# A fused attention and MLP-mixer kernel on one core: six reloaded weight slots, 56 score blocks, small passes on GpSimd, and a first chunk in half-chunks

## The chip, the core and the metric

The kernel runs on one core of a Trainium2 chip. The core has five engines, each with its own queue: TensorE (PE; its weight loads are listed apart as PEld), VectorE (DVE), ScalarE (ACT), GpSimd (POOL) and SyncE (SP, which here only issues DMAs). PE writes to eight PSUM banks of 128x512 float32 each; the other engines read these and work in SBUF. The metric is the device time of one execution in microseconds, the median of several.

## What is computed

One input x (2048 tokens of 512 features, bfloat16) goes through an attention block (a) and an MLP-mixer block (b); a sigmoid gate per token mixes the two.

```python
def reference(A_x, A_wqkv, A_wo, B_x, B_w1, B_w2, B_w3, B_w4, gate_w):
    ...
        scores = jnp.einsum("bhqd,bhkd->bhqk", q, k) * (Dh ** -0.5)
        p = _softmax(scores, axis=-1)
        o = jnp.einsum("bhqk,bhkd->bhqd", p, v)
        return (lambda x, *d: x.transpose(*d))(o, 0, 2, 1, 3).reshape(B, S, D) @ wo
    ...
        h = _gelu(_layernorm(x, axis=-1) @ w1)
        ...
        hs = jnp.concatenate([g0, g1, g2, g3], axis=-1) @ w2
        x1 = x + hs
        h2 = _gelu(_layernorm(x1, axis=-1) @ w3) @ w4
        return x1 + h2
    ...
    g = _sigmoid((x * gate_w).sum(-1, keepdims=True))
    a = _A_ref(x, A_wqkv, A_wo)
    b = _B_ref(x, B_w1, B_w2, B_w3, B_w4)
    return g * a + (1 - g) * b
```

There are 32 heads of 16 features. g0 to g3 are the four quarters of h, shifted by 1, -1, 2 and -2 tokens. w3 is 512x1792, w4 is 1792x512.

## The kernel before, in words

The 2048 query tokens are four chunks of 512. A round is one chunk, one group G of eight heads and one parity p: four heads at a time, one on each strip of 32 rows of PE. A round has 64 score blocks: 16 key tiles of 128 tokens for each of four heads, each block 128 keys by 512 queries, made by one matmul (L1482) with kT as its weights and q as the moving side. q is kept twice, with the odd heads zeroed (scaled by mE) and with the even heads zeroed (scaled by mO), since two heads share a strip. There are 32 rounds, 2048 blocks in all.

Each block must become exp(score). There are two ways. On ACT (`issue_act`, L1565) an exponential reads two or three PSUM banks at once and writes bfloat16 to `prob`, a pool of 40 slots of 128x512 (L1577). On DVE (`issue_dve`, L1589) the block is scaled and rounded to an integer whose bits are a rough exponential (L1609); three copies of it with a constant added to the bits (the shift passes) follow, on DVE (L1652) or GpSimd (L1654), and four PV matmuls, with V or with V scaled, add up to a better one. So a block costs PE one PV matmul (L1707) if it went to ACT and four if it went to DVE.

The projections and the MLP are cut into matmuls on four strips of 32 columns (L1112, from `gen`) and are fed between the score blocks. The results are copied out of PSUM by DVE (`evac`). Layernorm is bn_stats on DVE (L1284), a power on GpSimd, a normalising pass xn on DVE (L1304), a write to DRAM (L1308) and transposing DMAs back (L1314). GELU runs on ACT in three places (L1324): once over the whole of hT, and twice over hB and hT for a pair of chunks; each needs a table load there and one back.

The order of all this is worked out in the kernel while it is built. `Sim` holds a model of the engines and hands out work by priorities, buffers and planned positions, all counted in score blocks (`at`, the P_ constants, and STEPS, a table of parameters that can change every 8 blocks). What comes out is a fixed program for each engine; on the chip, the engines wait for one another by semaphores only, and each keeps its order. Buffers come from pools: `w` has nine slots of 128x4x512 for transposed x, the k and v weights, w1, w2, w3 (four slots), w4 (four slots) and the last outputs `ybuf`; wo has a tile of its own. `port=True` marks work that the planner keeps from overlapping between DVE and GpSimd; GpSimd then also waits for the last such DVE instruction.

The steps that the change touches: the loads of x and of the weights (`start`, `wload`, `load_xT`), the first chunk's transposes, q and k (`x_transposes`, `k_first`, `q_proj`), the q copies in `q_proj` (L1210), xn in `normalise`, the gate scaling of x_sb in `mlp2_up` (L1366), w3 and w4 in `mlp2_up` and `mlp2_down`, and the tail behind the last PV matmul (L2052 to L2103).

## Time and profile before

| | us |
|---|---|
| median of 3 runs (lowest, highest) | 735.15 (734.89, 735.43) |
| the profiled execution | 735.27 |
| its span in the profile | 733.3 |
| DMA: HBM read, written | 17.40 MB, 6.81 MB |
| granted TensorE clock | 0.999 |

In the groups of instructions a line gives the line of the code, the engine, the operation, what it writes and reads with shapes, the count, then the engine's busy time and the mean duration of one in ns, then the idle time of the engine just before them and what ended it. Neighbouring instructions of an engine overlap in the records, so busy time divided by the count is less than the mean duration. A line of the timeline gives start, duration, engine, line and the number of instructions merged into it. A line of the waits gives total time, number of waits and the longest. A line of the stretches gives for each engine the busy time and the number of instructions, then the granted clock, the DMA engines' share and GB/s.

### The profile page before, as it was taken

The numbers are of one execution on the slowest core, as the hardware profiler recorded it, in microseconds if no ns is written. First come the engines' busy times: TensorE is split into PE (matmuls) and PEld (weight loads), VectorE is DVE, ScalarE is ACT, GpSimd is POOL, SyncE is SP. The second block draws the span as 40 slices with busy tenths as digits, with TensorE's granted clock in tenths as the row PEclk, the third lists the DMA queues.
The fourth block names the chain that finished last, engine by engine and source line by source line (L and its number), as shares of the span: only waits on it lengthen the run. The fifth ranks groups of instructions, "written<-read, shape, count | busy, mean of one in ns | idle before, by whom it ended". The sixth has DMA issues, their size and how long they took to land.

```text
span 733.3 us, 23826 instructions
## 1 busy us (share of the span) xinstructions
PE 723.8 (99%) x9517; PEld 212.3 (29%) x9518; DVE 698.6 (95%) x1493; ACT 720.0 (98%) x751; POOL 452.7 (62%) x452
## 2 busy tenths in 40 slices
PE   9999999999999999999999999999999999999997
PEld 5434322222222222222322222222222232222222
DVE  6999999999999999999999999999999999999997
ACT  7999999999999999999999999999999999999995
POOL 3456685778867666658545555566576765575442
PEclk9999999999999999999999999999999999999999
DMA  8504223111212033024100100001100010000001
GB/s 189 162 19 77 80 66 71 28 45 57 72 49 53 21 96 69 21 81 96 32 25 10 46 28 21 27 23 43 27 20 18 7 32 24 28 26 19 14 22 41
DMA packets 67094, 34.60 MB, mean 47 GB/s; under 512 B 46748, under 2 KB 62380, under 8 KB 66984
## 3 DMA queue, kind: packets, MB, share of 16 engines
q1 hardware_dynamic: 66040, 32.56, 17.7%
q8 instruction: 74, 1.21, 0.7%
q10 hardware_dynamic: 944, 0.52, 0.2%
q14 instruction: 36, 0.29, 0.2%
HBM read 17.40 MB, written 6.81 MB: 33 GB/s over the span
## 4 chain that ended last, share of the span: by engine, by line
PE 64%; ACT 11%; DVE 4%; issue 2%; POOL 0%; ACTq 0%; DVEq 0%
PE banks L1707 24%; PE banks L1482 22%; PE banks L1112 17%; ACT prob L1577 6%; ACT hT L1324 2%; ACT hB L1324 2%; DVE prob L1609 1%; DVE prob L1652 1%; ACT L1324 1%; DVE x_sb L1357 0%; ACT L1326 0%; DVE st L1284 0%; DVE w L1415 0%; POOL prob L1654 0%; PE banks L2060 0%
## 5 line engine op out<-in xcount | busy, mean ns | idle before, releaser
L1577 ACT ACTIVATE prob<-banks 128x1024 bf16<-128x1024 f32 (+1 forms) x728 | 675.5, 1102 | 1.1 <-PE banks L1482 0.2
L1654 POOL TENSOR_SCALAR prob<-prob 128x1024 uint16<-128x1024 uint16 x390 | 400.3, 1045 | 233.4 <-DVE prob L1652 110.9
L1609 DVE TENSOR_SCALAR prob<-banks 128x512 uint16<-128x512 f32 x577 | 380.3, 684 | 17.4 <-PE banks L1482 12.9
L1707 PE MATMUL banks<-prob,V 128*17 128x512 bf16 (+1 forms) x3785 | 321.6, 381 | 0.2
L1482 PE MATMUL banks<-q,kT 32*128 32x512 bf16 x2048 | 280.1, 384 | 1.5 <-ACT prob L1577 0.7
L1652 DVE TENSOR_SCALAR prob<-prob 128x1024 uint16<-128x1024 uint16 x480 | 179.5, 422 | 2.0 <-PE banks L1707 0.6
L1482 PEld LDWEIGHTS <-kT 32*128 32x128 bf16 x2048 | 70.0, 90 | 295.3 <-ACT prob L1577 269.2
L1707 PEld LDWEIGHTS <-V 128*17 128x17 bf16 (+1 forms) x3785 | 71.8, 88 | 116.7 <-issue 94.9
L1112 PE MATMUL banks<-xnT,w 128*32 128x512 bf16 x1152 | 89.4, 383 | 0.0
L1112 PE MATMUL banks<-w,hT 128*32 128x512 bf16 x688 | 64.5, 384 | 0.0
L1746 POOL TENSOR_TENSOR oT<-accsb,bcs 128x512 bf16<-128x512 f32 x31 | 39.5, 1273 | 26.7 <-DVE prob L1652 21.5
L1112 PEld LDWEIGHTS <-w 128*32 128x32 bf16 x1936 | 41.0, 95 | 48.9 <-issue 27.0
L1112 PE MATMUL banks<-w,w 128*32 128x256 bf16 (+1 forms) x784 | 41.5, 308 | 0.4 <-DVE prob L1609 0.4
L1112 PE MATMUL banks<-w,hB 128*32 128x512 bf16 x448 | 36.0, 382 | 0.6 <-ACT hB L1324 0.6
L1123 PE MATMUL banks<-wo,oD 32*128 32x512 bf16 x64 | 24.6, 384 | 0.0
L1112 PEld LDWEIGHTS <-hT 128*32 128x32 bf16 x688 | 15.9, 95 | 20.5 <-issue 15.1
L1284 DVE BATCH_NORM_STATS2 st<-x_sb 128x6 f32<-128x512 bf16 x32 | 21.5, 678 | 0.0
L1728 DVE COPY accsb<-banks 128x512 f32<-128x512 f32 x31 | 21.1, 680 | 0.2 <-PE banks L1707 0.2
L1112 PE MATMUL banks<-wo,oD 128*32 128x512 bf16 x176 | 21.0, 384 | 0.0
L1112 PE MATMUL banks<-w,wq 128*32 128x512 bf16 x256 | 19.4, 382 | 1.0 <-DVE accsb L1728 1.0
L1378 DVE CAST hB<-banks 128x512 bf16<-128x512 f32 x28 | 19.0, 682 | 0.9 <-PE banks L1112 0.9
L1324 ACT ACTIVATE hT<-hT 128x7168 bf16<-128x7168 bf16 (+1 forms) x3 | 19.4, 6452 | 0.0
(94 smaller groups left out, 246.8 us busy)
## 6 DMA issues: line engine op xcount, KB each, us to landing
bcs<-rr SPq DMA_DIRECT2D x124, 64.0 KB
xn_dram<-xn SPq DMA_DIRECT2D x32, 128.0 KB
w<-in_B_w_dram SPq DMA_DIRECT2D x5, 512.0 KB
oD<-oT SPq DMA_DIRECT2D x124, 16.0 KB
w<-in_B_w_dram SPq DMA_DIRECT2D x4, 448.0 KB
out_dram<-ot SPq DMA_DIRECT2D x14, 128.0 KB
x_sb<-in_A_x_dram SPq DMA_DIRECT2D x3, 512.0 KB
w<-in_A_wqkv_dram SPq DMA_DIRECT2D x2, 256.0 KB
```

The costliest lines, as they stand in the source:

```text
L1112: units.append([Op("col", j, lambda j=j, lf=lf, rf=rf, n0=n0, n1=n1, st=st, sp=sp: nc.tensor.matmul(get()[32 * j:32 * j + 32, n0:n1], lhsT ...
L1123: o = Op("row", i, lambda: nc.tensor.matmul(get(), lhsT=lf(0, P)[rows], rhs=rf()[rows], start=False, stop=True, tile_position=(32 * i, 0), ...
L1284: a = dve(600, deps, lambda: nc.vector.bn_stats(out=sb.slot[:], in_=x_sb[:, t, :]), prio=6, at=at, acq=[sb])
L1324: g = nc.scalar.activation(out=ap, in_=ap, func=ACT.Gelu_apprx_tanh)
L1482: o = Op("row", i, lambda: nc.tensor.matmul(dst(), lhsT=kT[G][32 * i:32 * i + 32, kt * P:(kt + 1) * P], rhs=qbuf[G, c].slot[32 * i:32 * i ...
L1577: job = act(hold, ops, lambda: nc.scalar.activation(out=prob[:, pb.cut(), :].bitcast(BF16), in_=unit()[:, rb.cut(), :], func=ACT.Exp, scal ...
L1609: return nc.vector.tensor_scalar(out=prob[:, b0.cut() if w == 2 else b0.bufs[h0].slot, :], in0=unit()[:, rb.cut() if w == 2 else rb.bufs[0 ...
L1652: return nc.vector.tensor_scalar(out=cut(k), in0=cut(0), scalar1=float(SHIFT * k), scalar2=None, op0=ALU.add)
L1654: return nc.gpsimd.tensor_scalar(out=cut(k), in0=cut(0 if both else 2), scalar1=1.0, scalar2=float(SHIFT * (k if both else 1)), op0=ALU.mu ...
L1707: return nc.tensor.matmul(one(accs[r])[32 * i:32 * i + n, :], lhsT=lhs(n), rhs=rhs(), start=st and not edge, stop=True, tile_position=(0, ...
L1728: e = dve(PSUM_NS, round_ops[r], lambda: nc.vector.tensor_copy(out=ab.slot[:], in_=one(accs[r])), acq=[ab], prio=0, frees=[accs[r], Call(a ...
L1746: n = gp(1250, d3, lambda: nc.gpsimd.tensor_tensor(out=ob.slot[:], in0=ab.slot[:], in1=bb.slot[:], op=ALU.mult), acq=[ob], frees=[ab, bb], ...
```

## The change

1. `w` has six slots in place of nine, `prob` 56 in place of 40. wo moves into a `w` slot, loaded late; w2 is loaded late; w3 and w4 are loaded once for each pair of chunks and not once for all, so that they take turns in four slots; `ybuf` moves into an `xnT` slot.
2. The two q copies of each q projection (30), the xn passes (32) and the gate scalings of x_sb (14) move from DVE to GpSimd.
3. x's first chunk comes in four loads of one row tile each, two on SP and two on ACT, where there were two loads of two. A new function `first` does its transposes, copies, q and k in halves of 256 tokens by hand, with k and q on the whole array and not on four strips, after nine warm-up matmuls in place of eleven.
4. In the tail the matmuls on known data all stand behind the last PV matmul, the last four row tiles of the output leave from one `w` slot, the first two of them in one DMA.
5. Assumed latencies of DMAs and GELUs in the planner, planned positions and the table STEPS are others. In the program that comes out, ACT has 657 exponentials of two blocks and 48 of three (715 and 13 before), DVE 590 blocks (579), GpSimd 364 shift passes (390).

```diff
-    P_W1 = (143, 440)
+    P_W1 = (195, 445)
...
-    P_W3 = ((610, 710), (710, 840), (1200, 1390), (1400, 1570))
+    P_W3 = ((610, 710), (710, 840), (1245, 1400), (1410, 1570))
...
-    P_LD = (450, 888)
+    P_LD = ((450, 1190), (845, 1575))
...
-    NPROB, NTOK, NW = 40, 3, 9
+    NPROB, NTOK, NW = 56, 5, 6
...
-    xa, xb = (start(e, 3000.0, lambda q, a=a: q.dma_start(out=x_sb[:, a:a + 2, :], in_=x_src(0, a, a + 2)))
-              for e, a in (("SP", 0), ("ACT", 2)))
-    j_x0 = [xa, xb]
+    j_x0 = [start(("SP", "ACT")[a % 2], 3000.0, lambda q, a=a: q.dma_start(out=x_sb[:, a, :], in_=x_flat[a * P:(a + 1) * P, :]))
+            for a in range(4)]
...
-        dl_w[name] = dma(4000.0, [], fn, acq=[wslot(name, users)], prio=2)
+        dl_w[name] = dma(6300.0, [], fn, acq=[b], prio=2)
...
-    dl_w["o"] = dma(4000.0, [], lambda: nc.sync.dma_start(out=wo[:], in_=wrows(A_wo)), prio=2)
+    dl_w["2"].at = 330
+    wload("o", A_wo, 10 ** 6)
+    dl_w["o"].at = 855
...
-        for _ in range(11):
+        for _ in range(9):
...
+    def first(t):
...
+        def project(b, w, n0):
+            for k in range(KT):
+                guard(b, nc.tensor.matmul(one(b)[:, 0:256], lhsT=w[:, k, 0:P], rhs=W("x00")[:, k, n0:n0 + 256], start=k == 0,
+                                          stop=k == KT - 1, skip_group_check=True))
+
+        def mm():
+            parts = [(bt[0], 0, 0, 2), (bt[1], 0, 2, 4), (bt[2], 2, 0, 2), (bt[3], 2, 2, 3), (bt[4], 2, 3, 4)]
+            for i, (b, t0, k0, k1) in enumerate(parts):
+                for k in range(k0, k1):
+                    for u in range(2):
+                        guard(b, nc.tensor.transpose(
+                            out=one(b).bitcast(BF16)[:, (k - k0) * 256 + u * P:(k - k0) * 256 + (u + 1) * P],
+                            in_=x_sb[:, t0 + u, k * P:(k + 1) * P], identity=idb[:]))
+            for i, (b, t0, k0, k1) in enumerate(parts):
+                cp = nc.scalar.copy if i in (1, 3) else nc.vector.tensor_copy
+                sim.readers[b] = [cp(out=W("x00")[:, k0:k1, t0 * P:(t0 + 2) * P], in_=one(b).bitcast(BF16)[
+                    :, 0:(k1 - k0) * 256].rearrange("p (k c) -> p k c", c=256))]
+            project(bq[0], wq, 0)
+            nc.scalar.activation(out=qb.slot[:, 0, 0:256], in_=one(bq[0])[:, 0:256], func=ACT.Copy, scale=mE[:])
+            project(ba, W("k"), 0)
+            sim.readers[ba] = [nc.vector.tensor_copy(out=kT[0][:, 0:256], in_=one(ba)[:, 0:256])]
+            project(bq[1], wq, 256)
+            nc.vector.tensor_scalar(out=qb.slot[:, 0, 256:512], in0=one(bq[1])[:, 0:256], scalar1=mE[:], scalar2=None,
+                                    op0=ALU.mult)
+            project(bb, W("k"), 256)
...
-            j_q[G, c, p] = dve(262, [e, j_m3] + ([j_q[G, c, 0]] if p else []), lambda p=p, m=m: nc.vector.tensor_scalar(
-                out=qb.slot[:, p, :], in0=qf.slot[:], scalar1=m[:], scalar2=None, op0=ALU.mult), prio=0.3, port=True,
+            j_q[G, c, p] = gp(690, [e, j_m3] + ([j_q[G, c, 0]] if p else []), lambda p=p, m=m: nc.gpsimd.tensor_scalar(
+                out=qb.slot[:, p, :], in0=qf.slot[:], scalar1=m[:], scalar2=0.0, op0=ALU.mult, op1=ALU.add), prio=0.3,
                 acq=[] if p else [qb], frees=[qf])
...
-            g = dve(323, [m], lambda t=t, xb=xb: nc.vector.tensor_scalar(
+            g = gp(750, [m], lambda t=t, xb=xb: nc.gpsimd.tensor_scalar(
                 out=xb.slot[:], in0=x_sb[:, t, :], scalar1=rs[which][:, t:t + 1], scalar2=nm[which][:, t:t + 1],
...
-            jx1g[t] = dve(262, [last[t % 4], jgate], lambda t=t: nc.vector.tensor_scalar(
...
+            jx1g[t] = gp(700, [last[t % 4], jgate], lambda t=t: nc.gpsimd.tensor_scalar(
...
-    for i in range(KT):
-        wload(f"3{i}", B_w3[i * P:(i + 1) * P, :], NCH * FT)
...
+    for cs, at3, at4 in zip(PAIRS, *P_LD):
+        for i in range(KT):
+            wload(f"3{i}", B_w3[i * P:(i + 1) * P, :], 2 * FT)
+            dl_w[f"3{i}"].prio, dl_w[f"3{i}"].at = 6, at3 + 10 * i
+        for i in range(4):
+            wload(f"4{i}", B_w4[512 * i:min(F, 512 * (i + 1)), :], 8)
+            dl_w[f"4{i}"].prio, dl_w[f"4{i}"].at = 7, at4 + 10 * i
         mlp2(cs, s2, at_of, gate_job)
...
     for tt in (1, 3):
-        add_y(tt, tt not in early)
-    for tt in range(4):
-        if tt not in early:
-            known(tt, range(LG, 4), tt % 2 == 0)
+        into(tt, idf[:], y_of(tt), True)
+        known(tt, False)
+        known(tt - 1, True)
...
-        (nc.scalar if tt == 3 else nc.sync).dma_start(out=out_flat[t * P:(t + 1) * P, :], in_=o[:])
+        if tt == 1:
+            nc.sync.dma_start(out=out_flat[(t - 1) * P:(t + 1) * P, :].rearrange("(t p) d -> p t d", p=P), in_=both[:, 0:2, :])
+        elif tt > 1:
+            (nc.scalar if tt == 3 else nc.sync).dma_start(out=out_flat[t * P:(t + 1) * P, :], in_=o)
```

819 lines of the change are left out of this document (413 added, 406 removed).

## The prediction

> **What bounds the kernel now.** I read the busy times first. Four engines look full, so busy time alone decides nothing.
>
> ```profile
> PE 723.8 (99%) x9517; PEld 212.3 (29%) x9518; DVE 698.6 (95%) x1493; ACT 720.0 (98%) x751; POOL 452.7 (62%) x452
> ```
>
> Then the groups of instructions, for ScalarE (ACT). Its exponentials are one line of code in two widths, 1024 columns (two score blocks) and 1536 (three).
>
> ```profile
> L1577 ACT ACTIVATE prob<-banks 128x1024 bf16<-128x1024 f32 (+1 forms) x728 | 675.5, 1102 | 1.1 <-PE banks L1482 0.2
> L1577 ACT ACTIVATE prob<-banks 128x1024 bf16<-128x1024 f32 x715 | 659.7, 1095 | 0.8 <-PE banks L1482 0.2 <-DVE prob L1652 0.2 <-ACT prob L1577 0.2
> L1577 ACT ACTIVATE prob<-banks 128x1536 bf16<-128x1536 f32 x13 | 19.3, 1487 | 0.2
> L1324 ACT ACTIVATE hB<-hB 128x7168 bf16<-128x7168 bf16 x2 | 12.4, 6177 | 0.0
> L1324 ACT ACTIVATE hT<-hT 128x8192 bf16<-128x8192 bf16 x1 | 7.0, 7032 | 0.0
> ```
>
> Before 728 exponentials ACT is idle for 1.1 us in all. Busy can still hide waiting, so I checked the rate in stretches without a GELU, then who waits for whom, then the two ends.
>
> ```profile
> 200.00:300.00 100.00, 99.92 (x1291) 27.62 (x1287) 96.85 (x213) 99.84 (x109) 68.89 (x70) 1.00 0.23 56
> 400.00:500.00 100.00, 99.92 (x1266) 26.61 (x1263) 97.59 (x209) 99.84 (x109) 56.15 (x53) 1.00 0.11 30
> PEld L1482 <- ACT prob L1577: 269.2, 645, 0.8
> 8.54 8.28 ACT L1577 ACTIVATE prob<-banks 128x1536 bf16<-128x1536 f32 x7
> 715.83 8.82 ACT L1577 ACTIVATE prob<-banks 128x1024 bf16<-128x1024 f32 x9
> 728.71 0.69 ACT L2099 ACTIVATE ot<-banks,omg 128x512 bf16<-128x512 f32 x1 [4.06 <-PE banks L2060]
> ```
>
> In a stretch the engines stand in the order PE, weight loads, DVE, ACT, POOL, each with its count. Both stretches, 200 us apart, hold 109 ACT instructions, one per 100/109 = 0.917 us: a steady rate. The score matmuls of TensorE (PE, L1482) wait for the exponentials to give banks back, 645 times; ACT hardly ever waits for PE. So ACT sets the pace from 8.54 to 715.83 + 8.82 = 724.65 us. The span is three parts: 8.54 until the first exponential, 716.1 of ACT, 733.3 - 724.65 = 8.65 of tail. That the chain of waits is 64% PE doesn't contradict this: it is followed to an instruction's neighbour on its own engine where nothing releases it, and PE always has a neighbour.
>
> **ACT's new share of the score blocks.** There are 2048 blocks of 128x512. Before, ACT does 715 x 2 + 13 x 3 = 1469 and VectorE (DVE) 579. The instruction list of the changed kernel has 657 exponentials of two blocks and 48 of three: 657 x 2 + 48 x 3 = 1458 blocks in 705 instructions; DVE gets 590. An exponential costs blocks times a slope plus a fixed part. Slope, first way, from the two GELU widths: (7032 - 6177)/1024 x 512 = 428 ns a block; the fixed part is then (675.5 - 1469 x 0.428)/728 = 64 ns; after, 1458 x 0.428 + 705 x 0.064 = 669.1 us, 6.4 less. Second way, from the widths of the exponentials: 1487 - 1095 = 392 ns a block, fixed part 137 ns, after 668.1, 7.4 less. The GELU rows are free of the overlap between neighbours, so I take -6.4. The GELUs and table loads stay the same in number. Lower bound of the gain: 715 x 0.917 + 13 x 1.345 = 673.1, so 2.4 us of the 675.5 are already stalls; if these double the gain is 4.0.
>
> **What DVE gives and takes.** Removed are 32 normalising passes, 30 for q, 14 that scale x. Added are 11 blocks and, with GpSimd's share cut from 390 to 364 passes, 44 shift passes of 1024 columns (477 to 521).
>
> ```profile
> L1609 DVE TENSOR_SCALAR prob<-banks 128x512 uint16<-128x512 f32 x575 | 377.8, 682 | 17.4 <-PE banks L1482 12.9 <-POOL prob L1654 0.4 <-issue 0.3
> L1609 DVE TENSOR_SCALAR prob<-banks 128x1024 uint16<-128x1024 f32 x2 | 2.4, 1222 | 0.0
> L1652 DVE TENSOR_SCALAR prob<-prob 128x1024 uint16<-128x1024 uint16 x477 | 178.9, 423 | 2.0 <-PE banks L1707 0.6
> L1304 DVE TENSOR_SCALAR xn<-x_sb,rs,nm 128x512 bf16<-128x512 bf16 x32 | 12.1, 404 | 1.1 <-DMA xn_dram<-xn 1.1
> L1210 DVE TENSOR_SCALAR q<-qf,mO 128x512 bf16<-128x512 bf16 x15 | 5.3, 350 | 0.0
> L1366 DVE TENSOR_SCALAR x_sb<-x_sb,omg 128x512 bf16<-128x512 bf16 x14 | 4.2, 344 | 0.0
> ```
>
> -12.1 - 2 x 5.3 - 4.2 = -26.9. Score passes: 575 to 564 single ones at 377.8/575 = 0.657 and 2 to 13 double ones at 1.2: -7.2 + 13.2 = +6.0. Shifts: 44 x 178.9/477 = +16.5. Sum -4.4: 694 us of DVE in a span some 6 us shorter, 95% as before. It pays for the moved blocks and stays as tight as it was.
>
> **GpSimd (POOL).** It loses 26 shifts and gains 76 passes of 512 columns.
>
> ```profile
> L1654 POOL TENSOR_SCALAR prob<-prob 128x1024 uint16<-128x1024 uint16 x390 | 400.3, 1045 | 233.4 <-DVE prob L1652 110.9 <-PE banks L1482 31.2 <-PE banks L1707 24.1
> L1293 POOL TENSOR_SCALAR rs<-mv 128x4 f32<-128x4 f32 x8 | 1.5, 193 | 6.5 <-DVE prob L1652 3.9 <-DVE xn L1304 1.7 <-DVE mv L1285 0.6
> L1746 POOL TENSOR_TENSOR oT<-accsb,bcs 128x512 bf16<-128x512 f32 x31 | 39.5, 1273 | 26.7 <-DVE prob L1652 21.5 <-DMA bcs<-rr 3.1 <-DVE nm L1297 1.1
> ```
>
> No row has such a pass. It costs between half of 1045 (0.52 us) and the 1.27 us of a two-input pass of that width: 76 x 0.52 - 26 x 1.03 = +13 to 76 x 1.27 - 26 x 1.03 = +70 us on 452.7. I take 0.62, between the one-input rows of 4 and 1024 columns (0.193 + 508 x 0.852/1020): +20, 65% of the span. Even the upper end is no bound; what can cost is that q and xn come later behind shifts in POOL's queue, under cover of the blocks of the round that runs.
>
> **PE.** PV matmuls go from 3785 to 3818, fillers from 12 to 28 (they stand beside the GELUs, where PE has nothing else), row pieces from 80 to 64.
>
> ```profile
> L1707 PE MATMUL banks<-prob,V 128*17 128x512 bf16 (+1 forms) x3785 | 321.6, 381 | 0.2
> L1123 PE MATMUL banks<-wo,oD 32*128 32x512 bf16 x64 | 24.6, 384 | 0.0
> L1112 PE MATMUL banks<-w,hT 128*32 128x512 bf16 x688 | 64.5, 384 | 0.0
> L2040 PE MATMUL banks<-zero 128*17 128x384 bf16 x12 | 1.2, 327 | 0.0
> ```
>
> The first chunk's matmuls are in the start, below. 33 x 0.085 = +2.8; 16 x 0.1 = +1.6; 16 row pieces at 0.384 become column pieces at 64.5/688 = 0.094: -4.6. Sum -0.2: nothing, and PE waits for ACT anyway.
>
> **Weight reloads.** w3 and w4 are now loaded once for each pair of chunks, into slots that the other has just left. Cover, counted in score blocks of PE's list, at 716.1/2048 = 0.35 us each: from the last read of w4 to the first w3 matmul of the second pair 55 blocks, 19 us; from the last read of w3 to the first w4 matmul 25 to 35 blocks, some 8 us, and a GELU.
>
> ```profile
> 336.69 0.58 SPq L1061 DMA_DIRECT2D w<-in_B_w_dram  x1
> 338.00:340.00 2.00, 2.00 (x30) 0.52 (x27) 1.98 (x5) 1.98 (x3) 1.92 (x3) 1.00 0.69 226
> 590.68 1.28 ACT L1324 ACT_TABLE_LOAD   x1
> SPq L1738 <- DVE prob L1652: 54.1, 14, 10.9
> ```
>
> A load begins about 1.4 us after its issue and moves 226 GB/s. Four of 448 KB need 1.8 MB/226 GB/s = 8 + 1.4 + the issue: 10 us, against 19, and against 8 + 1.28 + 6.2 (the first GELU) = 15 us, after which ACT has another 6.2 + 1.28 of its own to do. I cost the reloads at nothing; without the cover, 10 us each. The 8 issues more on SP (0.5 us each) stand in a queue that is mostly waiting.
>
> **Start.** Before, the chain is: warm-up matmuls, transposes, copies, q and k, their copies, first scores.
>
> ```profile
> 1.12 3.70 PE L1091 MATMUL banks<-zero 128*128 128x384 bf16 x11 [1.12 <-DVE zero L1080]
> 4.62 1.45 PE L1143 MATMUL banks<-idb,x_sb 128*128 128x128 bf16 x16
> 6.00 1.14 PE L1112 MATMUL banks<-w,wq 128*32 128x512 bf16 x16
> 5.29 1.18 ACT L1155 COPY w<-banks 128x512 bf16<-128x512 bf16 x2 [1.99 <-PE banks L1143]
> 7.62 0.42 DVE L1169 CAST kT<-banks 128x256 bf16<-128x256 f32 x1 [1.09 <-PE banks L1112]
> ```
>
> Two warm-up matmuls fewer are 2 x 3.70/11 = 0.67 us, if x is there: it was by 4.62, when nothing but the warm-up held PE, and how much earlier no row shows. The halves let copies start after eight transposes, but q's second half and k's first now go through DVE one behind the other (two of 0.42). From the first transpose to the first exponential I count 1.45 + 0.3 (rest of the copies) + 1.2 (three half projections, partly behind copies) + 2 x 0.42 + 0.4 (scores) = 4.2 against 8.54 - 4.62 = 3.9. So 0.3 late if x is not there sooner, 0.67 - 0.3 = 0.4 early if it is, 0.7 if the copies hide; I take 0.4. Far end: the warm-up ran 384 columns in 0.34 us, the q projection 512 in 1.14/4 = 0.29. Sixteen matmuls of 256 columns at the warm-up's rate cost 16 x 0.22 = 3.6, at twice it 1.8: another 1.8 late.
>
> The Trainium skill (TensorE: Matmul & The Clock Gate, Part 1) says the array runs at half its clock until about 3.4 us of sustained work; the two rates of this trace agree, the warm-up of now gives 3.7 us of work and the shorter one only 3.0, so by the rule the 1.8 would be due and the sum 730.7.
>
> **Tail.** Two of the output's rows of tiles leave in one DMA.
>
> ```profile
> 725.41 1.98 PE L2060 MATMUL banks<-w,idf 128*128 128x512 f32 x4
> 729.16 0.74 DVE L2101 SCALAR_TENSOR_TENSOR xn<-banks,omg,w 128x512 bf16<-128x512 f32 x1
> 730.20 0.40 SPq L2103 DMA_DIRECT2D out_dram<-xn  x1
> ```
>
> The third issue waits today from 729.90 (its data) to 730.20: up to 0.3 gained. Two more matmuls on known data move behind the last PV: up to 2 x 0.29 = 0.6 lost, if the wait for DVE's transposes does not hide them. Zero.
>
> **Sum.** The profiled execution took 735.27 (span 733.3 and 2.0 around it), 0.1 above the median. 735.27 - 6.4 - 0.4 = 728.5 us. Own range: 735.27 - 7.4 - 0.7 - 0.3 = 726.9 to 735.27 - 4.0 + 1.8 + 0.6 = 733.7.
>
> **Rivals.**
> 1. *PE is the bound after all.* For it: 99% busy, the chain. Then ACT's 6.4 us are worth nothing: -0.2 and the start's -0.4, 734.7. Against: 269.2 us of waiting for ACT.
> 2. *DVE becomes the bound,* by its sum alone: 735.27 - 4.4 - 0.4 = 730.5, which lies in the own range. ACT's short idle speaks against it.
> 3. *The GpSimd passes block DVE* (slower). Place: all the 76 new passes.
>
> ```profile
> L1652 DVE TENSOR_SCALAR prob<-prob x480: 278/418/1035, 13.2 to 723.6; 128x1024 uint16<-128x1024 uint16 x159, 128x512 uint16<-128x512 uint16 x1
> ```
>
> A shift has taken 1035 ns, a whole POOL pass, where the median is 418: a DVE pass on SBUF data can be held for a POOL pass. If each new one held DVE for its 0.62 us, 76 x 0.62 = 47 us; DVE has 733.3 - 698.6 = 35 idle and would be 12 over: 728.5 + 12 = 740. It decides from 35/76 = 0.46 us a pass. Against: the mean, 423, is 5 ns over the median, so 477 shifts beside 390 POOL passes lost some 2 us in all.
>
> The Trainium skill (SBUF — State Buffer, Who interferes with whom) states that lock as exclusive for a whole instruction, for whichever comes second; the 1035 agrees, the mean says that the order of the two engines mostly avoids it.
> 4. *A reload comes late* (slower). Place: w4's loads between the last w3 matmul and the GELUs, stuck on SP behind an issue that waits for DVE, 10.9 at the longest. 10 + 10.9 = 21 us against 15 + 7.5 before ACT is out of work and, for w3, 19. PE's queue would hold everything behind the first w4 matmul. A wait at its longest gives 2 of stall for w3 alone; twice that long, on all three, (32 - 22.5) x 2 + (32 - 19) = 32. A middle case, 9 us in all, gives 737.5. It costs from a delay of 9 us on (w3) and turns the sign from some 8 us of stall.
>
> **How the numbers follow.** No change can be told within 0.2% (1.5 us). Forecast 0.74, rival 2 0.05, rival 1 0.07, rival 3 0.05, rival 4 0.09. Faster: 0.74 + 0.05 = 0.79; same 0.07; slower 0.14. Own range 726.9 to 733.7; taken up to rival 1's 734.7 and a little below, 726.5 to 735.0, it leaves the slower cases and small tails out, under 2 in 10.
>
> **What will show it.** ACT: 705 exponentials at 669 us, idle before them near 1 us, 0.917 us each in calm stretches. First exponential near 8.2. DVE near 694, POOL near 473, the shift mean still near 423 (rival 3: over 500). PE without waits on weight loads near blocks 1358 and 1683. Wrong would be: ACT idle or stretched by over 6 us, above all beside the GELUs or where q comes from POOL.

## The result, and the profile after

The changed kernel takes 731.81 us against 735.29 for the kernel before, measured beside it: a ratio of 0.995, with a 95% interval of 0.9935 to 0.9965. Its runs lie between 730.81 and 732.28; a further one, at a TensorE clock of 0.66, is left out of the comparison. The profiled execution took 731.34 with a span of 729.4, 3.9 us shorter than the span before. I forecast 728.5, from 726.5 to 735.0.

First the page's busy times, and then, from the groups of instructions, ScalarE's exponentials, the shift passes and the moved passes (busy time, mean ns of one | idle time before them).

```profile
PE 719.9 (99%) x9533; PEld 214.3 (29%) x9533; DVE 698.0 (96%) x1461; ACT 713.2 (98%) x728; POOL 481.0 (66%) x502
```

```profile
L1631 ACT ACTIVATE prob<-banks 128x1024 bf16<-128x1024 f32 (+1 forms) x705 | 669.1, 1121 | 3.1 <-PE banks L1536 2.8
L1706 DVE TENSOR_SCALAR prob<-prob 128x1024 uint16<-128x1024 uint16 x521 | 192.3, 423 | 3.6 <-POOL prob L1708 2.3 <-PE banks L1761 0.4 <-DVE prob L1706 0.2
L1358 POOL TENSOR_SCALAR xn<-x_sb,rs,nm 128x512 bf16<-128x512 bf16 x32 | 25.0, 785 | 13.8 <-DVE prob L1706 3.7 <-DVE V L1284 3.1 <-DVE nm L1351 1.8
L1264 POOL TENSOR_SCALAR q<-qf,mO 128x512 bf16<-128x512 bf16 x15 | 10.4, 695 | 9.5 <-DVE prob L1706 9.5
```

The 705 exponentials take 669.1 us, 6.4 less than before. But ACT is now idle for 3.1 us before them, where it was 1.1. Of that, 2.8 is ended by score matmuls. So 2.0 us of what ACT saved are stalls. That it still sets the pace is tested below.

The start, from the timeline (start, duration, engine, line, operation, count, idle time before it):

```profile
3.97 1.91 PE L1206 MATMUL banks<-idb,x_sb 128*128 128x128 bf16 x16
6.28 0.61 PE L1198 MATMUL banks<-w,wq 128*128 128x256 bf16 x4 [0.39 <-DMA wq<-in_A_wqkv_dram]
6.73 0.60 PE L1198 MATMUL banks<-w,w 128*128 128x256 bf16 x4
8.78 1.45 ACT L1631 ACTIVATE prob<-banks 128x1536 bf16<-128x1536 f32 x1 [0.17 <-PE banks L1536]
```

The transposes begin at 3.97 in place of 4.62, but the 16 take 1.91 in place of 1.45, and PE then waits for q's weights. The first exponential stands at 8.78, 0.24 later than the 8.54 before; among the profiles below that have this start it stands between 8.61 and 9.53, so the 0.24 is one draw from a wide spread. The end, from the timeline:

```profile
600.58 119.96 ACT L1631 ACTIVATE prob<-banks 128x1024 bf16<-128x1024 f32 x129
719.78 1.05 POOL L1708 TENSOR_SCALAR prob<-prob 128x1024 uint16<-128x1024 uint16 x1 [4.25 <-ACT prob L1631]
721.50 0.72 DVE L2122 STREAM_TRANSPOSE accsb<-banks 128x512 f32<-128x512 f32 x1 [1.60 <-PE banks L1761]
```

The last exponential ends at 600.58 + 119.96 = 720.54, so the tail is 729.4 - 720.54 = 8.86 in place of 8.65. GpSimd makes the last shift, until 720.83; the last PV matmuls stand behind it, and VectorE waits 1.60 us for them. The four differences add up: -6.4 (exponentials) + 2.0 (idle) + 0.24 (start) + 0.2 (tail) = -4.0, and the spans differ by 3.9.

Of the 3.1 us of idle time 2.4 lie in one place, which I call the pocket. This is the timeline there, all engines:

```profile
82.20 1.27 POOL L1800 TENSOR_TENSOR oT<-accsb,bcs 128x512 bf16<-128x512 f32 x1 [2.37 <-DMA bcs<-rr]
...
87.66 2.02 POOL L1358 TENSOR_SCALAR xn<-x_sb,rs,nm 128x512 bf16<-128x512 bf16 x2 [1.15 <-DMA xn_dram<-xn]
...
89.65 1.04 POOL L1708 TENSOR_SCALAR prob<-prob 128x1024 uint16<-128x1024 uint16 x1
...
90.75 0.39 PE L1761 MATMUL banks<-prob,V 128*17 128x512 bf16 x2 [1.19 <-POOL prob L1708]
...
91.97 0.25 DVE L1789 RECIPROCAL pk<-pk 128x16 f32<-128x16 f32 x1 [0.81 <-DMA pk<-den]
...
92.36 1.02 ACT L1631 ACTIVATE prob<-banks 128x1024 bf16<-128x1024 f32 x1 [1.14 <-PE banks L1536]
...
92.97 0.94 PE L1761 MATMUL banks<-prob,V 128*17 128x512 bf16 x10 [0.33 <-DVE prob L1706]
...
94.27 1.02 ACT L1631 ACTIVATE prob<-banks 128x1024 bf16<-128x1024 f32 x1 [0.89 <-PE banks L1536]
```

ACT's two gaps, 1.14 and 0.89, are ended by score matmuls (L1536); a third, of 0.37, ends at 95.67. These wait for nothing themselves: they stand in PE's queue behind PV matmuls (L1761) that wait for a shift pass, once GpSimd's and once VectorE's. GpSimd's shift at 89.65 stands behind two xn passes. They had waited for one of the two xn places, which a DMA frees, and everything there came late already since oT had waited 2.37 for its broadcast. VectorE, too, had a shift that waited 2.29 for GpSimd's. Its next shift stands behind a reciprocal that waits for the DMA pk. The DMA queue of SP shows why these DMAs are late:

```profile
71.18 5.68 SPq L1368 DMA_TRANSPOSE xnT<-xn_dram  x4
76.97 2.58 SPq L1796 DMA_DIRECT2D bcs<-rr  x4
79.59 3.13 SPq L1804 DMA_DIRECT2D oD<-oT  x4
...
84.47 2.41 SPq L1804 DMA_DIRECT2D oD<-oT  x4
86.98 0.54 SPq L1784 DMA_DIRECT2D den<-accsb  x1
...
89.38 0.38 SPq L1786 DMA_DIRECT2D pk<-den  x1
```

Up to 87.5 it is nearly without a gap. The second broadcast (bcs) stands behind four transposes, and den, whose data VectorE had copied by 83.5, behind four oD stores; pk, which reads den, comes behind it.

### The profile page after: what moved, and what is told of

Same layout as the page of the kernel before. It is cut to its first block, busy times and chain, and to the rows that moved or that the text cites. A ratio compares the mean times of both kernels' runs of the same rounds, so it can differ in the third digit from the quotient of the medians.

```text
span 729.4 us, 23745 instructions
## 1 busy us (share of the span) xinstructions
PE 719.9 (99%) x9533; PEld 214.3 (29%) x9533; DVE 698.0 (96%) x1461; ACT 713.2 (98%) x728; POOL 481.0 (66%) x502
## 3 DMA queue, kind: packets, MB, share of 16 engines
q1 hardware_dynamic: 68472, 36.23, 19.7%
## 4 chain that ended last, share of the span: by engine, by line
PE 80%; ACT 13%; DVE 2%; issue 2%; DMA 1%; POOL 1%; SPq 0%; ACTq 0%; DVEq 0%
PE banks L1761 29%; PE banks L1536 26%; PE banks L1134 24%; ACT prob L1631 12%; ACT hT L1378 1%; DVE prob L1706 1%; DMA wq<-in_A_wqkv_dram 1%; DMA xn_dram<-xn 1%; DVE prob L1663 0%; PE banks L2111 0%; POOL prob L1708 0%; ACT L1378 0%; DVE hB L1431 0%; PE banks L1291 0%; PE banks L1198 0%
## 5 line engine op out<-in xcount | busy, mean ns | idle before, releaser
L1631 ACT ACTIVATE prob<-banks 128x1024 bf16<-128x1024 f32 (+1 forms) x705 | 669.1, 1121 | 3.1 <-PE banks L1536 2.8
L1708 POOL TENSOR_SCALAR prob<-prob 128x1024 uint16<-128x1024 uint16 x364 | 374.5, 1047 | 180.7 <-DVE prob L1706 118.5
L1663 DVE TENSOR_SCALAR prob<-banks 128x512 uint16<-128x512 f32 (+1 forms) x577 | 385.0, 693 | 12.7 <-PE banks L1536 8.0
L1761 PE MATMUL banks<-prob,V 128*17 128x512 bf16 (+1 forms) x3818 | 319.6, 381 | 2.1 <-POOL prob L1708 1.5
L1536 PE MATMUL banks<-q,kT 32*128 32x512 bf16 x2048 | 275.7, 384 | 1.4 <-ACT prob L1631 0.2
L1706 DVE TENSOR_SCALAR prob<-prob 128x1024 uint16<-128x1024 uint16 x521 | 192.3, 423 | 3.6 <-POOL prob L1708 2.3
L1536 PEld LDWEIGHTS <-kT 32*128 32x128 bf16 x2048 | 69.1, 90 | 289.0 <-ACT prob L1631 265.5
L1761 PEld LDWEIGHTS <-V 128*17 128x17 bf16 (+1 forms) x3818 | 73.5, 88 | 120.0 <-issue 96.4
L1134 PE MATMUL banks<-w,hT 128*32 128x512 bf16 x696 | 57.6, 383 | 0.0
L1134 PE MATMUL banks<-w,w 128*32 128x256 bf16 (+1 forms) x752 | 38.0, 309 | 0.0
L1358 POOL TENSOR_SCALAR xn<-x_sb,rs,nm 128x512 bf16<-128x512 bf16 x32 | 25.0, 785 | 13.8 <-DVE prob L1706 3.7
L1145 PE MATMUL banks<-w,oD 32*128 32x512 bf16 x56 | 21.5, 384 | 0.0
L1134 PE MATMUL banks<-w,oD 128*32 128x512 bf16 x184 | 21.0, 384 | 0.1
```

What stands on the lines that cost most here:

```text
L1134: units.append([Op("col", j, lambda j=j, lf=lf, rf=rf, n0=n0, n1=n1, st=st, sp=sp: nc.tensor.matmul(get()[32 * j:32 * j + 32, n0:n1], lhsT ...
L1145: o = Op("row", i, lambda: nc.tensor.matmul(get(), lhsT=lf(0, P)[rows], rhs=rf()[rows], start=False, stop=True, tile_position=(32 * i, 0), ...
L1358: g = gp(750, [m], lambda t=t, xb=xb: nc.gpsimd.tensor_scalar(out=xb.slot[:], in0=x_sb[:, t, :], scalar1=rs[which][:, t:t + 1], scalar2=nm ...
L1536: o = Op("row", i, lambda: nc.tensor.matmul(dst(), lhsT=kT[G][32 * i:32 * i + 32, kt * P:(kt + 1) * P], rhs=qbuf[G, c].slot[32 * i:32 * i ...
L1631: job = act(hold, ops, lambda: nc.scalar.activation(out=prob[:, pb.cut(), :].bitcast(BF16), in_=unit()[:, rb.cut(), :], func=ACT.Exp, scal ...
L1663: return nc.vector.tensor_scalar(out=prob[:, b0.cut() if w == 2 else b0.bufs[h0].slot, :], in0=unit()[:, rb.cut() if w == 2 else rb.bufs[0 ...
```

## The experiments

Each time below is the median of several runs (two for the run without the reloads), with the ratio to the kernel before, run beside it, and the ratio's 95% interval. The changed kernel's ratio was 0.995 (0.9935 to 0.9965), so two kernels whose times differ by less than some 1.5 us can't be told apart by their medians; the profiles tell more, with one execution each.

### The xn places, the start and the tail, one at a time

The first edit gives the first layernorm's xn tiles eight places in hB, which is free then, in place of two slots.

```diff
...
+            xs = lambda t=t, xb=xb: xb.slot[:] if which else hB[:, (t % 8) * D:(t % 8 + 1) * D]
...
-                out=xb.slot[:], in0=x_sb[:, t, :], scalar1=rs[which][:, t:t + 1], scalar2=nm[which][:, t:t + 1],
+                out=xs(), in0=x_sb[:, t, :], scalar1=rs[which][:, t:t + 1], scalar2=nm[which][:, t:t + 1],
```

> The first layernorm's normalised tiles go into eight places in hB, which is idle then, in place of two xn slots; every engine keeps its order. Theory A (of the 6.4 us that ACT's smaller share is worth, 2.0 are given back in one pocket at 90 to 96 us: an xn pass on GpSimd waits for the write to DRAM that frees its slot, the shift behind it in GpSimd's queue comes late, the PV matmul that needs it holds TensorE, ACT runs dry): the idle before exponentials falls from 3.1 to under 1.2 us, the span from 729.4 to about 727.4, the time to about 729.3. Rival B (GpSimd is late there because its passes are long, 785 ns for xn, not because of the slot): the idle stays near 3 us and the span within 0.5 us of 729.4.

Measured: 731.78 us, 0.9942 (0.9928 to 0.9957), idle before exponentials 2.8. The timeline of this kernel in the pocket:

```profile
92.45 1.02 ACT L1632 ACTIVATE prob<-banks 128x1024 bf16<-128x1024 f32 x1 [0.48 <-PE banks L1537]
92.46 0.25 DVE L1790 RECIPROCAL pk<-pk 128x16 f32<-128x16 f32 x1 [1.22 <-DMA pk<-den]
...
94.77 1.02 ACT L1632 ACTIVATE prob<-banks 128x1024 bf16<-128x1024 f32 x1 [1.29 <-PE banks L1537]
```

The first gap shrank from 1.14 to 0.48 and the second grew from 0.89 to 1.29, with the reciprocal's wait for pk, 1.22 in place of 0.81. That the xn places alone make the pocket fell: where one queue is let go, the other is what ends last. From the first exponential to the end of the last it is 711.44 us in place of 711.76. The six times lie between 729.24 and 732.96, so a small gain could be hidden in them. The idle time fits the rival, but its cause, long passes, is not shown by this.

The second edit issues q's and k's first weights ahead of x's third and fourth row tile.

```diff
...
+    first_loads = [xl(0), xl(1), col(wq, 0, 128), col(W("k"), D, D + 128)]
...
+    dl_w["q0"] = start("SP", 2600.0, xl(2))
+    dl_w["k0"] = start("ACT", 2900.0, xl(3))
```

> Same four loads of x, but the loads of the first 128 columns of the q and k weights are issued second on each queue and the second row tiles third. Theory A (the start is late because wq is issued behind two row tiles: TensorE waits 0.66 us for it): the q matmuls no longer wait for wq, the first exponential moves from 8.78 to 8.2 to 8.5 us, the span falls by 0.3 to 0.5. Rival B (the DMA engines are the limit at the start, whatever the order): what wq gains the second row tiles lose, the first exponential stays within 0.15 of 8.78.

Measured: 733.18 us, 0.9962 (0.9947 to 0.9976). The timeline of its start:

```profile
5.83 1.03 PE L1207 MATMUL banks<-idb,x_sb 128*128 128x128 bf16 x8 [0.79 <-DMA x_sb<-in_A_x_dram]
6.65 1.06 PE L1199 MATMUL banks<-w,wq 128*128 128x256 bf16 x4
7.50 1.06 PE L1199 MATMUL banks<-w,w 128*128 128x256 bf16 x4
...
10.44 2.37 ACT L1632 ACTIVATE prob<-banks 128x1536 bf16<-128x1536 f32 x2
```

Now PE waits for x. Beyond that, groups of four matmuls follow one another after 7.50 - 6.65 = 0.85 us, where the changed kernel shows 6.73 - 6.28 = 0.45: PE ran at half rate here until past 9 us. The first exponential comes 1.7 late. My expectation that this order saves the wait was wrong, and the rival, with the first exponential within 0.15 of 8.78, was wrong too. Some of the 1.7 may be chance: when PE goes over to full rate differs between profiles (last section).

The third edit gives the last shift pass of all to VectorE.

```diff
...
-                return nc.gpsimd.tensor_scalar(out=cut(k), in0=cut(0 if both else 2), scalar1=1.0,
+                return (nc.vector if (id(bufs), k) == pool_shifts[-1] else nc.gpsimd).tensor_scalar(out=cut(k), in0=cut(0 if both else 2), scalar1=1.0,
```

> Only the last shift pass of the kernel runs on VectorE in place of GpSimd, at the same place in the order. Theory A (the tail is 0.2 us longer than before because the last PV matmuls wait for a GpSimd pass of 1.05 us): the tail from the last exponential's end to the span's end falls from 8.86 to about 8.3 us. Rival B (the last PV matmuls are held by the last exponential itself): the tail stays within 0.15 of 8.86.

Measured: 731.19 us, 0.994 (0.9927 to 0.9953), span 728.9. From its timeline:

```profile
699.62 20.88 ACT L1631 ACTIVATE prob<-banks 128x1024 bf16<-128x1024 f32 x21
...
719.78 0.42 DVE L1710 TENSOR_SCALAR prob<-prob 128x1024 uint16<-128x1024 uint16 x1
721.06 0.72 DVE L2126 STREAM_TRANSPOSE accsb<-banks 128x512 f32<-128x512 f32 x1 [0.86 <-PE banks L1765]
```

The shift takes 0.42 in place of 1.05, VectorE waits 0.86 in place of 1.60, and the tail is 728.9 - (699.62 + 20.88) = 8.4, 0.46 shorter. That one pass cost more than the 0.2 that the tail had lost.

### What the moved passes are worth

Here the 32 xn passes go back to VectorE; the order of the program stays.

```diff
-            g = gp(750, [m], lambda t=t, xb=xb: nc.gpsimd.tensor_scalar(
+            g = gp(750, [m], lambda t=t, xb=xb: nc.vector.tensor_scalar(
```

> Undoes one part of the move: the 32 normalising passes run on VectorE again, at the same place in the order; the rest as changed. Theory A (the pocket comes from xn passes standing ahead of shifts in GpSimd's queue while they wait for a slot; VectorE has no 12 us to spare without ACT noticing): the pocket at 90 to 96 us shrinks or moves to VectorE, VectorE's busy time goes up by 12 us to about 710, and stalls of ACT elsewhere grow: the span is 729 to 733. Rival B (moving xn to GpSimd was a loss as such): the span falls by 2 us or more below 729.4.

Measured: 741.58 us, 1.0081 (1.0067 to 1.0094), slower than the kernel before. One row from the busy times' part of the page, one from the groups of instructions and one from the view of the tile xn (min/median/max of one in ns):

```profile
PE 725.4 (98%) x9532; PEld 216.2 (29%) x9533; DVE 711.6 (96%) x1493; ACT 716.7 (97%) x728; POOL 455.7 (62%) x470
```

```profile
L1631 ACT ACTIVATE prob<-banks 128x1024 bf16<-128x1024 f32 (+1 forms) x705 | 672.6, 1106 | 10.5 <-PE banks L1536 7.5 <-PE banks L1761 2.1 <-issue 0.2
```

```profile
L1358 DVE TENSOR_SCALAR xn<-x_sb,rs,nm x32: 392/413/1395, 38.0 to 264.2; 128x512 bf16<-128x512 bf16 x32
```

VectorE is busy for 13.6 us more, ACT is idle for 7.4 us more and its exponentials take 3.5 more, and the span grows by 10.8. I had put this version at 729 to 733, so VectorE has less slack than I thought: most of what it gets more turns up in the span. Two causes are mixed in this. The passes took 19.7 us here (614 ns each) where they took 12.1 before (404 ns each), so part of the 13.6 is passes that were held up, and not their work. And the loss is local: the last xn pass starts at 264.2, and from 344.46 on the same 272 exponentials take the same 252.26 us as in the changed kernel. In this order the new share of the score blocks could not be had with these passes on VectorE; an order planned for that was not tried. One xn pass, where the order does not keep it apart from GpSimd's, took up to 1395 ns here, where the median is 413; with the planned order of before the longest was 591. The Trainium skill (SBUF — State Buffer, Who interferes with whom) states that VectorE and GpSimd hold each other for a whole instruction on shared access; the 1395 agrees with a wait for GpSimd's shift, which takes 1045.

### Does ACT set the pace, and do the reloads cost anything

For the first question 88 exponentials of one column were added on ACT, one ahead of every eighth.

```diff
...
+            if more[0] % 8 == 0:
+                nc.scalar.activation(out=dump, in_=zero[:, 0:1], func=ACT.Exp)
```

> One more one-column exponential on ACT before each eighth exponential: 88 of them, 0.11 us each by the ones behind the GELUs, 9.7 us of ACT in all. If ACT sets the pace: the time goes up by 9 to 10 us. If VectorE sets it at least as much (taking 13 us of passes back to VectorE cost 10): ACT has slack wherever VectorE holds, and the time goes up by less than 6.

Measured: 737.45 us, 1.0036 (1.0023 to 1.0048). The busy times of the page:

```profile
PE 724.4 (98%) x9533; PEld 214.0 (29%) x9533; DVE 699.7 (95%) x1461; ACT 719.7 (98%) x816; POOL 481.1 (65%) x502
```

ACT is busy for 719.7 - 713.2 = 6.5 us more, and the span of 735.7 is 6.3 longer. I had priced one at 0.11 us, it was 6.5/88 = 0.074; the exchange is one for one. By the medians it is 737.45 - 731.81 = 5.6, and 6.3 by the ratios. These lie below the 9 to 10 that I expected only because the instruction is cheaper; the test is the exchange. That ACT sets the pace, the step on which my -6.4 rests, is shown. VectorE is close behind, as the run with xn on it showed.

For the second question the second loading of w3 and of w4 is left out, so that the second pair of chunks multiplies with what the slots then hold.

```diff
...
+            if again:
+                return
```

> Leaves out the second loading of w3 and w4, so that the second pair of chunks is computed with whatever weights lie in the slots. By the prediction's term (reloads cost nothing): the stretch from 400 us to the last exponential keeps its length within 0.3 us, and no wait of TensorE near the second pair's w3 and w4 goes away because there was none. Rival (a reload is late and TensorE waits): that stretch gets shorter by 1 us or more.

Measured: 731.29 us, 0.9947 (0.9928 to 0.9965). Two rows of its timeline, which begin behind the two pairs of GELUs:

```profile
333.73 252.26 ACT L1637 ACTIVATE prob<-banks 128x1024 bf16<-128x1024 f32 x272
...
600.95 119.96 ACT L1637 ACTIVATE prob<-banks 128x1024 bf16<-128x1024 f32 x129
```

The changed kernel's row of the first stretch, with the reloads:

```profile
333.35 252.26 ACT L1631 ACTIVATE prob<-banks 128x1024 bf16<-128x1024 f32 x272
```

272 exponentials take 252.26 us in both, and the last 129 take 119.96 in both (the changed kernel's row stands in the section on the result). The reloads cost nothing.

### The pocket

First I moved all four transposes of the second chunk behind pk of the third round in SP's queue.

```diff
...
+    later = max(t for t, n, fn in sim.order if getattr(fn, "tag", None) == ("pk", 2))
+    sim.order = [(later + 1e-3, n, fn) if getattr(fn, "tag", None) == ("xnT", 0, 1) else (t, n, fn)
+                 for t, n, fn in sim.order]
```

> One move in SP's queue: the four transposing loads of the normalised second chunk (5.7 us of issue, first used some 27 us later) go behind the second and third rounds' softmax bookkeeping (broadcast bcs, oD, den, pk) in place of ahead of it. Theory C (the pocket at 90 to 96 us is SP's queue: behind these transposes the broadcast of 1/sum comes late, so GpSimd's oT waits 2.4 us with shifts behind it, and den and pk come late, so VectorE's reciprocal waits 0.8 us with shifts behind it; TensorE's PV and ACT follow): the oT wait near 82 us and ACT's idle at 90 to 96 us go (idle before exponentials from 3.1 to under 1.2 us), and from the first exponential to the last the time falls from 711.8 to about 709.8 us; the median falls by 1.5 to 2. Rival D (the pocket is GpSimd's own load, six xn and q passes and shifts too many in that stretch): the oT wait goes but ACT's idle stays over 2 us.

Measured: 732.62 us, 0.9967 (0.9955 to 0.9979). Its profiled execution, with ACT idle for 7.0 us, took 735.44, where the other five lie between 732.29 and 733.14, so the sizes of its gaps are its own. The timeline there:

```profile
74.97 1.27 POOL L1805 TENSOR_TENSOR oT<-accsb,bcs 128x512 bf16<-128x512 f32 x1 [3.75 <-DMA bcs<-rr]
...
78.34 18.21 ACT L1634 ACTIVATE prob<-banks 128x1024 bf16<-128x1024 f32 x19 [1.55 <-POOL prob L1711]
98.70 1.02 ACT L1634 ACTIVATE prob<-banks 128x1024 bf16<-128x1024 f32 x1 [2.15 <-POOL prob L1711]
```

The second oT's wait near 82 is gone, but the first oT now waits 3.75 for its broadcast, and the transposes, later now, stand among the next round's DMAs. ACT's gaps of 1.55 and 2.15 both end on GpSimd's shift. The stall moved, and by the medians nothing was gained. Two loads of two row tiles came next, as in the kernel before, with the rest of the new start kept.

```diff
...
+    x2 = lambda a: (lambda q: q.dma_start(out=x_sb[:, a:a + 2, :], in_=x_src(0, a, a + 2)))
+    first_loads = [x2(0), x2(2), lambda q: None, lambda q: None]
```

> The first chunk of x in two loads of two row tiles, as before the change, so that the q and k weights are issued 0.45 us earlier; all else as changed. Theory A (the start is late because the q weights land late, 6.2 us and more, behind four loads): TensorE does not wait for wq, and the first exponential comes at 8.2 to 8.5 us, against 8.78 to 9.53 in the runs with four loads. Rival B (both row tiles come later as one load, the transposes start late and the clock is lost): the first exponential at 9 us or later.

Measured: 731.15 us, 0.9944 (0.993 to 0.9957). From its timeline:

```profile
5.58 0.60 PE L1199 MATMUL banks<-w,wq 128*128 128x256 bf16 x4
...
8.07 4.62 ACT L1632 ACTIVATE prob<-banks 128x1536 bf16<-128x1536 f32 x4 [0.17 <-PE banks L1537]
...
95.59 4.83 ACT L1632 ACTIVATE prob<-banks 128x1024 bf16<-128x1024 f32 x5 [0.37 <-PE banks L1537]
```

PE doesn't wait for q's weights, and the first exponential comes at 8.07, 0.71 sooner than with four loads. But behind the pocket ACT goes on at 95.59, and at 95.67 in the changed kernel: 0.08 of the 0.71 is left. The second oT stands at 82.26 (82.20 in the changed kernel), having waited 3.02 for its broadcast in place of 2.37, and ACT's idle time is 3.9 in place of 3.1. So the waits on DMAs set the pocket's end, and a sooner start is spent waiting there.

Then the order of SP's queue again, by less: only the third and fourth transpose go behind the second broadcast. bcs has one place, so the broadcast can't go before the first oT has read it, at 74.1; two transposes fit ahead of that.

```diff
...
+    later = max(t for t, n, fn in sim.order if getattr(fn, "tag", None) == ("bcs", 1))
+    sim.order = [(later + 1e-3, n, fn) if getattr(fn, "tag", None) == ("xnT", 0, 1, 1) else (t, n, fn)
+                 for t, n, fn in sim.order]
```

> The order of SP's queue between 70 and 82 us alone differs: the third and fourth transpose of the second chunk's normalised rows stand behind the four broadcasts (bcs) of the second round, where all four stood ahead of them. bcs has one place, so the second broadcasts can go from the end of the first product oT (74.1 us) on; in the changed kernel they went only at 76.97. Theory A (SP's queue makes GpSimd late, and GpSimd the pocket): the second oT starts by 80 in place of 82.20, its wait of 2.37 falls below 1, ACT's idle time before exponentials falls from 3.1 to 1.0 to 2.0, the span from 729.4 to 727.8 to 728.6. Rival B (the pocket comes from other waits near 90 us, those for the third round's sums or for the later rows of xn): the wait for bcs falls too, but ACT's idle time stays between 2.5 and 3.5 and the span within 0.6 of 729.4. Rival C: the transposes, now 2.7 us later, are missed: PE waits for xnT, idle over 3.5.

Measured: 731.91 us, 0.995 (0.9938 to 0.9962), idle 3.5. Its timeline:

```profile
80.18 1.26 POOL L1805 TENSOR_TENSOR oT<-accsb,bcs 128x512 bf16<-128x512 f32 x1
...
87.41 2.43 POOL L1358 TENSOR_SCALAR xn<-x_sb,rs,nm 128x512 bf16<-128x512 bf16 x2 [2.49 <-DMA xn_dram<-xn]
```

oT comes 2.0 sooner and waits for nothing, yet xn now waits 2.49 for its place in place of 1.15, and the shift behind it stands at 89.81, where it stood at 89.65. Rival B had it, but for the span, 730.1, which is 0.7 longer after a start 0.35 later: the pocket has more waits than this one. Rival C fell, since PE doesn't wait for xnT longer than before. The same order with the two loads and the last shift on VectorE:

> The order of the run before, two loads of two row tiles for the first chunk, and the last GpSimd shift on VectorE, together. Theory A: the first exponential near 8.07, the tail near 8.4 (8.86 in the changed kernel), idle time before exponentials at most 2: the span 729.4 - 0.71 - 0.46 - (1 to 1.5) = 726.7 to 727.2, the time near 729. Rival B: the earlier start is eaten by the pocket, whose end stays near 95.6, and only the tail counts: 728.9, the time near 731.

Measured: 730.92 us, 0.9939 (0.9926 to 0.9953), span 729.1, idle 3.4. The first exponential comes at 8.12, and the last one ends at 720.59, in the changed kernel at 720.54: the start's gain was eaten again. What was left to suspect was three waits behind one another: bcs, the xn place, and pk behind den behind the oD stores. I took all three away at once, with the two loads and the last shift:

```diff
...
+    behind = {("xnT", 0, 1, 1): ("bcs", 1), ("oD", 1): ("pk", 2)}
+    tag_of = lambda fn: getattr(fn, "tag", None)
+    later = {a: max(t for t, n, fn in sim.order if tag_of(fn) == b) + 1e-3 for a, b in behind.items()}
+    sim.order = [(later.get(tag_of(fn), t), n, fn) for t, n, fn in sim.order]
```

> Five edits of order and place: the first layernorm's xn tiles in eight places of hB; the third and fourth transpose behind the second round's broadcasts; the four oD stores of the second round behind the pk store of the third (so that den and pk go some 2.4 us sooner); two loads of two row tiles; the last shift pass on VectorE. Theory D: the pocket is made of two queues in order, GpSimd's shift behind an xn pass that waits for a free place (and before that behind oT), and VectorE's shift behind a reciprocal that waits for pk, and pk behind den behind the oD stores. Both waits go: the reciprocal waits under 0.2 us for pk, PE's PV matmuls near 91 us wait under 0.3 for a shift, ACT's idle time before exponentials is 0.8 to 1.6 and the stretch between 80 and 100 us holds no gap over 0.4. With the first exponential near 8.1 and a tail of 8.4 the span is 729.4 - 0.71 - 0.46 - (1.5 to 2.3) = 725.9 to 726.7, the time 728 to 729, ratio near 0.991. Rival E (PE's own work in that stretch, 32 matmuls of w1 between two groups of scores, makes the pocket): idle stays over 2.5, the span 728 to 729, the time 730 to 731.

Measured: 729.12 us, 0.993 (0.9912 to 0.9948), span 726.4. The group of the exponentials, then rows of the timeline:

```profile
L1636 ACT ACTIVATE prob<-banks 128x1024 bf16<-128x1024 f32 (+1 forms) x705 | 669.3, 1119 | 0.7 <-PE banks L1541 0.4
```

```profile
53.19 57.06 ACT L1636 ACTIVATE prob<-banks 128x1024 bf16<-128x1024 f32 x58
...
83.90 0.55 SPq L1793 DMA_DIRECT2D den<-accsb  x1
...
85.70 1.04 POOL L1715 TENSOR_SCALAR prob<-prob 128x1024 uint16<-128x1024 uint16 x1
...
88.87 0.25 DVE L1800 RECIPROCAL pk<-pk 128x16 f32<-128x16 f32 x1 [0.49 <-DMA pk<-den]
```

58 exponentials run from 53.19 to 110 without a gap. GpSimd's shift comes at 85.70 in place of 89.65 and the reciprocal at 88.87 in place of 91.97. It still waits 0.49 for pk, more than the 0.2 I expected, but nothing on ACT's side hangs on that any more. The idle time is 0.7, so rival E fell, and this version has the lowest median of all, though two of its six times lie at 732.3 and 732.5. Against the run before it only the xn places and the oD stores are new: with them the idle time goes from 3.4 to 0.7 and the span from 729.1 to 726.4. Last, the three edits without the two loads and the last shift:

> The changed kernel with the three edits of order and place alone (xn tiles in hB, the transposes behind the broadcasts, the oD stores behind pk); its start and its tail are the changed kernel's. Theory D: ACT's idle time before exponentials at most 1.2 in place of 3.1, the span 729.4 - (1.9 to 2.4) = 727.0 to 727.5 if the first exponential stands at 8.78, as much later as it starts later (8.8 to 9.5 so far), the time 729 to 730. Rival F (the edits only pay with the earlier start): idle over 2, span over 728.5 at a start of 8.8.

Measured: 729.65 us, 0.9927 (0.9915 to 0.9938). The rows of the groups and of the timeline:

```profile
L1635 ACT ACTIVATE prob<-banks 128x1024 bf16<-128x1024 f32 (+1 forms) x705 | 669.7, 1120 | 1.4 <-PE banks L1540 0.8 <-POOL prob L1712 0.2
```

```profile
9.15 5.97 ACT L1635 ACTIVATE prob<-banks 128x1536 bf16<-128x1536 f32 x5 [0.17 <-PE banks L1540]
```

The idle time is 1.4 in place of 3.1, with a start 0.37 later than in the changed kernel's profile. So the edits pay alone too, by 731.81 - 729.65 = 2.2 us in the medians, though the two were not run side by side and the intervals of their ratios overlap; by the spans it is 0.7, after the later start. From the first exponential to the end of the last it is 710.58 us in place of 711.76, so 1.2 of the 1.7 us of idle time reach the end. Idle time and span both miss what I expected (at most 1.2; 727.0 to 727.5, and 0.4 more for the start).

## Why the prediction was right, and where it was wrong

**Direction and range: right.** Faster by 0.5%, inside the range, from the cause that I named. But of the 6.8 us forecast for the profiled execution 3.9 came: the exponentials gave what they should, and stalls, start and tail took 2.9 of it away. What in the change makes the new share possible, the 56 places of `prob`, the moved passes or the new positions, no run here takes apart, but for the xn passes.

**ACT's share: right.** 705 exponentials at 669.1 us were forecast and are there. The equal decimal is luck: with the fixed part not rounded to 64 ns the same sum gives 669.3, a gain of 6.2. The other way, 668.1, was 1.0 too low, so the sum bears out the slope from the two GELU widths better; one sum can't tell a slope from a fixed part. The added exponentials show that this time counts in full.

**The stalls: the term that was mis-sized, nothing in place of 2.0.** I had kept the idle time near 1 and put doubled stalls, 2.4 us, into the range only. Two steps were missing. "The 8 issues more on SP (0.5 us each) stand in a queue that is mostly waiting" holds for these eight, which cost nothing, and I looked at SP no further; but between 58 and 90 us the queue hardly waits, and what counts there is the order of four kinds of DMA. And on GpSimd I asked only whether q and xn come late behind shifts. It is the other way about: a shift comes late behind an xn that waits for its place, and the shift has PE's queue behind it, and the scores. The row of xn before, with 1.1 us of waiting for the place, named that wait already; on VectorE it cost less, and the change put it ahead of a shift pass. Taking the three waits away, with two loads at the start and the last shift on VectorE, gave 729.12, within 0.1% of the 728.5.

**The start: -0.4 forecast, +0.24 measured.** "Two warm-up matmuls fewer" did bring the transposes 0.65 forward, and with two loads 8.07 - 4.09 = 3.98 us from the first transpose to the first exponential come near the 4.2 that I counted. The step left out is that q's weights stand behind more loads: PE waits 0.39 for them. In the profiles with two loads the first exponential stands between 8.07 and 8.39, in those with four and the same order between 8.61 and 9.53. The far end of 1.8, q and k at half rate, is not seen in the changed kernel but in the run with the swapped weights; what ran at half rate in the changed kernel is the transposes, 1.91 us for 16, where 16 later ones, at 9.13, take 1.07. The Trainium skill (TensorE: Matmul & The Clock Gate, Part 1) has half rate end after about 3.4 us of sustained work; I had counted the warm-up's 3.06 us alone. The transposes behind it were still at half rate, and the groups of four from 6.28 on, 0.45 us apart, at full rate, which agrees with an end behind 3.06. Whether the transposes count as work no run here separates.

**The tail: 0 forecast, +0.2 measured, within its bounds.** One GpSimd shift in front of the last PV matmuls, worth 0.46 when VectorE makes it.

**VectorE and GpSimd.** 694 forecast, 698.0 measured; 473 forecast, 481.0 measured, since a pass of 512 columns costs 0.69 to 0.79 and not 0.62. Neither changed the time by its sum. But the run with xn on VectorE shows that "stays as tight as it was" meant little slack: 13.6 us more of busy time made the span 10.8 longer.

**The reloads: nothing, as forecast**, shown by leaving out the second loading.

**The rivals.** PE as the bound (734.7) fell: its weight loads still wait for the exponentials, and the time follows ACT one for one. VectorE as the bound gave 730.5, near the time measured, but for another reason; ACT's idle time in the pocket ends on waits, not on VectorE's sum, and goes to 0.7 with VectorE's work nearly the same. GpSimd's passes blocking VectorE (740) fell: the mean shift is 423 as before. The late reload fell with the run without it.

## What to carry to other kernels

In this tuned program one engine set the pace. What was taken off it came out within 0.2 us of the sum, and what was lost again was lost in a few places where queues in order hold something small. So list the idle gaps of that engine, and follow each back through the queues until a DMA or a free buffer is reached. Look at a DMA queue in the stretch in question, not over the span, and ask of each instruction that can wait what stands behind it. Where one wait is taken away and the time stays, look for the next one behind it before the theory is dropped: here two edits that were tried alone were worth next to nothing, and with a third the idle time fell from 3.1 to 1.4. The third was not tried alone, and no two of them without the other one.

## What I had not expected of the hardware

When PE goes over to full rate at the start is not fixed by the program. After the same nine matmuls (3.06 us) groups of four matmuls followed one another after 0.45 us in the changed kernel and after 0.85 in the run with the swapped weights, until past 9 us; PE had waited 0.39 in the one and 0.79 in the other shortly before. The run with xn in hB has the changed kernel's start:

```profile
3.98 1.16 PE L1206 MATMUL banks<-idb,x_sb 128*128 128x128 bf16 x16
6.97 0.61 PE L1198 MATMUL banks<-w,wq 128*128 128x256 bf16 x4 [1.84 <-DMA wq<-in_A_wqkv_dram]
```

Its 16 transposes take 1.16 us, where they take 1.91 in the changed kernel, near the 1.07 of 16 later ones there: it went over to full rate among them, the changed kernel behind them. PE then waited 1.84, and its next four matmuls take 0.61 as in the changed kernel, so that wait didn't bring half rate back. What sets the moment stays open. The Trainium skill (TensorE: Matmul & The Clock Gate, Part 1) states that activity is counted in a free-running window, so that the number of slow matmuls differs from run to run; that would allow all of this, but no run here shows the window. The landing of q's weights varies too with nothing changed in the loads: of kernels with the same start, the first exponential stands at 8.78 in the changed one, at 9.15 in the last run, and at 9.53 in this one, where the first q matmul came 0.69 later than at 6.28. One profile of a start is no measure of it to better than half a microsecond.
